# The early expert's remaining tokens as a float32 slot on weights already on chip

## The chip, the cores and the metric

The kernel runs on one core of a Trainium2 chip. The metric is device microseconds of one launch, the median of several runs. The core has five engines with a queue each: TensorE (PE; PEld is its weight load), VectorE (DVE), ScalarE (ACT), GpSimd (POOL) and SyncE (SP, which here only issues DMAs). Each engine works off its queue in order; semaphores between them keep the data right.

## The reference

Three stages follow each other, in float32:

1. Attention: 2 batches, 8 heads, 576 positions, head size 64, softmax over a causal window of 64. Its output, heads side by side, is x with 1152 rows of 512.
2. A mixture of 8 experts. Each token goes to the expert of its largest logit and is weighted by the probability of that choice; an expert takes at most 288 tokens, further ones give zero.
3. A dense layer pair: `h = x @ w_in`, `g = h * clip(h + 3, 0, 6) / 6`, `g @ w_out`, with 2048 hidden columns.

```python
logits = x @ w_gate
expert_idx = np.argmax(logits, axis=1)
...
h = np.maximum(np.einsum('ecd,edf->ecf', disp, w1), 0.0)   # w1: 8 x 512 x 1024
y = np.einsum('ecf,efd->ecd', h, w2)                       # w2: 8 x 1024 x 512
...
    if keep[i]:
        out[i] = gate_w[i] * y[expert_idx[i], pos[i]]
```

## The kernel before

**Early expert.** Attention goes over nine tiles of 128 tokens. After the first five, the expert that holds most tokens so far (the early expert) is chosen (`early_expert`, L722), and up to 128 of its tokens are computed while attention is still going on. Its weights are loaded whole into `wE`: four units of 256 hidden columns, each with a half of w1 and a half of w2 (512 KB each), in float32 as they come. A unit's work is an up product (four matmuls, `early_up`), ReLU on ACT, two transposes of the hidden rows (`early_hidden`), a copy on ACT, and a down product (two matmuls, `early_down`). Units 0 and 1 lie inside attention; units 2 and 3 follow it, in the loop from L1888.

**Slots.** When all tokens are known, the experts are ranked by the tokens they still have (`ranks`, L919; `keyB` takes the early expert's done tokens off its count), and eight slots with fixed capacities take them: ranks 0 to 2 hold 256, 224 and 208 tokens, ranks 3 to 5 hold 128, ranks 6 and 7 hold 64. `RANKS` says which rank each slot has. The early expert's remaining tokens are one of the ranks, and its weights are loaded again like any other's. Tokens are gathered from `x_dram` by GpSimd (`rows_of`, L790), scaled by their gate (`scale`, L1283), turned on TensorE and split into a high and a low part (`prep`).

**Precision.** Slots of 128 tokens and more, and the dense part, use float32r matmuls in three passes (`PASSES`): weights and data are split into high and low parts. Each quarter unit of weights takes a cast on ACT (L253) and a subtraction on DVE (L258). Slots of 64 take the weights as they are. The dense part's weights are converted first (`conv64`, two operations on ACT and four on DVE per piece).

**Stages and order.** The expert stage runs three teams of slots (`TEAMS`), each a large slot (`ws_stage`, weights stationary; a step `w` is half a unit) with one or two small ones (`ts_stage` or `tiny_stage`, steps `a` and `b`); the strings of `ORDER` give the order of the steps. The dense part then goes over four groups of tokens. A slot's finished rows are turned into the dense part's input `x2` by `to_dense`; `x2` has the memory in which `wE` lies before. Loads, casts, subtractions and conversions are jobs that a planner (`advance`, `fill`) puts into the queues wherever its estimates of the engines leave room; a ring of eight raw tiles and a ring of six split halves set how far ahead it goes. `FIRST_AT` and `SECOND_AT` say at which unit the four pieces of the dense part's first two units are loaded and converted. `compact_index` (L1749), which works out where each output row goes, is issued a few operations at a time (`aside`).

**PSUM.** Eight banks; transposes of tokens before the stage take banks 2 and 3 in turn (`t`), the short-lived products of the stage banks 0, 1 and 2 in turn (`rot`).

Of the kernel before, what the change touches and what calls it, by code (L numbers as in the profile page):

```python
# [15 lines left out]
AF = mybir.ActivationFunctionType  # L16
ALU = mybir.AluOpType
# [6 lines left out]
def tile_kernel(ctx, tc, q, k, v, w_gate, w1, w2, w_in, w_out, out, cap):  # L24
# [9 lines left out]

    RANKS = [3, 6, 0, 4, 1, 5, 7, 2]
    TEAMS = [((0, 1), 2), ((3,), 4), ((5, 6), 7)]
    NBIG = 3
    NTINY = 2  # L40
    BIG = (256, 224, 208)
    SCAP = [BIG[r] if r < NBIG else 128 if r < E - NTINY else 64 for r in RANKS]


    PAST = []
    for s, r in enumerate(RANKS):
        for part in range(SCAP[s] // 128, 3 if r <= NBIG else 2):
# [125 lines left out]
    FU = 256  # L173
# [101 lines left out]
    xTE = x2f[:, 2 * NFU * HALF : 2 * NFU * HALF + DM].rearrange("p (c t) -> p c t", c=NC)  # L275


    rt = ctx.enter_context(tc.tile_pool(name="rt", bufs=1))
# [34 lines left out]
    with ExitStack() as actx:  # L313
# [408 lines left out]
        def early_expert(e):  # L722
            ce, (k8, eq, t8, _), (mk, tE) = box["cE"], e8, e1
            at_ = place(0, NE, box["pE"])
            V.scalar_tensor_tensor(out=k8, in0=ce, scalar=8.0, in1=c_desc, op0=ALU.mult, op1=ALU.add)
            next(at_)
            V.tensor_reduce(out=mk, in_=k8, axis=AX.X, op=ALU.max)
            V.tensor_scalar_min(t8, ce, 128.0)
            next(at_)
            V.tensor_scalar(out=eq, in0=k8, scalar1=mk, scalar2=None, op0=ALU.is_equal)  # L730
            V.tensor_copy(et[0], pos[:, 0:NE])
            V.tensor_tensor(out=subE, in0=t8, in1=eq, op=ALU.mult)
            V.tensor_tensor(out=k8, in0=eq, in1=c_e, op=ALU.mult)
            V.scalar_tensor_tensor(out=keyB, in0=subE, scalar=-8.0, in1=c_desc, op0=ALU.mult, op1=ALU.add)
            V.tensor_reduce(out=tE, in_=k8, axis=AX.X, op=ALU.add)
            V.tensor_scalar_mul(nsub, subE, -1.0)
            V.tensor_copy(eI[:, 0:1], tE)
# [111 lines left out]
        def early_hidden_out(u):  # L849
            return lambda e: copy(e, box["hE"][:, early_part(u)], box["vE", u])  # L850
# [99 lines left out]

        def first_gather(e):
            box["x0"] = t = first_w[2]
            rows_of(t, sidx[:, 3 * RANKS[0] : 3 * RANKS[0] + 1])

        def gate_parts(e):
            V.tensor_reduce(out=gate, in_=ex, axis=AX.X, op=ALU.add)
# [877 lines left out]
    def ahead(step, *what):  # L1834
        prep_at.setdefault(step, []).append(what)

    rows_at = []
    for g, (small, b) in enumerate(TEAMS):
        st = start[False, small[0]]
        todo = [(small[0], 0, st - 3), (b, 0, st - 2), (b, 1, st - 1)]  # L1840
        if len(small) > 1:
            todo.append((small[1], 0, st))
        if g == 0:
            todo = [(b, 0, -1), (b, 1, -1), (small[1], 0, 0)]
        for s, i, at_step in todo:
            if g:
                ahead(at_step - 1, prep_scale, s, i)
            ahead(at_step, prep, s, i)
# [22 lines left out]
    xg[0, 0] = box["x0"]  # L1871

    def early_end(u, r):
        r = spend("PE", 0.22, r) + 0.2
        early_hidden(u)("PE")
        fill(r)
        early_hidden_out(u)("A")
        r = spend("A", 0.27, r) + 0.2
        if u >= NFU - 2:
            prep(TEAMS[0][1], u - NFU + 2, "t")  # L1880
        for i in range(2):
            early_down(u, i)("PE")
        r = spend("PE", 1.71, max(r, done["wl", u, 1])) + 0.2
        fill(r)
        return r

    before = None
    for u in range(NEU, NFU):  # L1888
        for i in range(2):
            early_up(u, i)("PE")  # L1890
        r = spend("PE", 1.71, done["wl", u, 0]) + 0.2
        fill(r)
        early_relu(u)("A")
        r = spend("A", 0.27, r) + 0.2
        if u == NEU:
            prep_scale(0, 0, done["g0"])
            prep(0, 0, "t")
            for n, (s, i, _) in enumerate(rows_at[:3]):
                prep_scale(s, i, done["g0"] + 2.2 * (n + 1))
        if before:  # L1900
            early_end(*before)
        before = u, r
    r = early_end(*before)
    early_out("A")
    r = spend("A", 0.52, r) + 0.2
    at(0, to_dense, box["yE"], None, r)
# [68 lines left out]
```

## Time and profile before

| | us |
|---|---|
| runs | 424.16, 425.08, 425.15 |
| median | 425.08 |
| profiled execution | 424.75 |
| its span | 423.0 |
| PE busy | 403.9 (95%) |
| DVE busy | 291.1 (69%) |
| ACT busy | 242.7 (57%) |

The span is the part that the profile covers, from the first instruction to the last; the rest of the execution lies around it. Busy time of TensorE includes the pipeline's modelled ends, so single matmuls overlap: the time that an operation takes of the engine is read from the start of one group to the start of the next. The rows further down are whole lines of the profile; L numbers are lines of this kernel.

### The profile page before, as it was taken

The numbers are of one execution on the slowest core, as the hardware profiler recorded it, in microseconds if no ns is written. First come the engines' busy times: TensorE is split into PE (matmuls) and PEld (weight loads), VectorE is DVE, ScalarE is ACT, GpSimd is POOL, SyncE is SP. The second block draws the span as 40 slices with busy tenths as digits, with TensorE's granted clock in tenths as the row PEclk, the third lists the DMA queues.
The fourth block names the chain that finished last, engine by engine and source line by source line (L and its number), as shares of the span: only waits on it lengthen the run. The fifth ranks groups of instructions, "written<-read, shape, count | busy, mean of one in ns | idle before, by whom it ended". The sixth has DMA issues, their size and how long they took to land.

```text
span 423.0 us, 8492 instructions
## 1 busy us (share of the span) xinstructions
PE 403.9 (95%) x3055; PEld 346.4 (82%) x3055; DVE 291.1 (69%) x801; ACT 242.7 (57%) x526; POOL 51.4 (12%) x108
## 2 busy tenths in 40 slices
PE   8999788889999999999999999999999999999992
PEld 5887665578898999988899999888888888898981
DVE  1988967568989999967679999548896222323430
ACT  3887773576769787736787576348573222422330
POOL 8633404200003001000000000000000000200111
PEclk9999999989999999999999999999999999999998
DMA  9998765997999998699810290032500000110101
GB/s 166 212 234 192 253 249 184 329 356 257 323 322 371 309 308 241 206 339 342 291 65 2 66 331 2 2 99 99 179 24 0 2 0 2 50 50 2 50 27 56
DMA packets 67058, 69.69 MB, mean 165 GB/s; under 512 B 30816, under 2 KB 49248, under 8 KB 67008
## 3 DMA queue, kind: packets, MB, share of 16 engines
q1 hardware_dynamic: 65424, 63.99, 48.4%
q0 software_dynamic: 1584, 5.08, 3.4%
q8 instruction: 26, 0.43, 0.4%
q14 instruction: 24, 0.20, 0.2%
HBM read 64.34 MB, written 4.72 MB: 163 GB/s over the span
## 4 chain that ended last, share of the span: by engine, by line
PE 85%; DVE 5%; DMA 3%; ACT 2%; issue 2%; SPq 1%; POOL 1%; POOLq 0%; ACTq 0%; DVEq 0%
PE banks L239 71%; DMA raw<-in_moe_w_dram 3%; PE banks L496 2%; PE banks L1482 2%; PE banks L1457 2%; PE banks L614 2%; DVE neg L573 1%; PE banks L560 1%; PE banks L596 1%; PE banks L653 1%; PE banks L1419 1%; ACT pe L586 1%; PE banks L1293 1%; PE banks L526 1%; DMA x_dram<-xt 0%
## 5 line engine op out<-in xcount | busy, mean ns | idle before, releaser
L258 DVE TENSOR_TENSOR wt<-raw,wt 128x512 fp32r<-128x512 f32 x116 | 74.9, 685 | 9.2 <-ACT wt L253 8.8
L239 PE MATMUL banks<-x,wt 128*128 128x320 f32 (+3 forms) x432 | 79.8, 336 | 0.0
L239 PEld LDWEIGHTS banks<-x,wt 128*128 128x128 f32 x432 | 70.8, 188 | 7.1
L253 ACT CAST wt<-raw 128x512 fp32r<-128x512 f32 x116 | 68.0, 630 | 9.5 <-DMA raw<-in_moe_w_dram 5.8
L239 PE MATMUL banks<-wt,g 128*128 128x512 f32 x288 | 69.6, 390 | 0.0
L1546 DVE SCALAR_TENSOR_TENSOR gf<-r,banks 128x320 f32<-128x320 f32 (+3 forms) x48 | 26.6, 554 | 60.2 <-ACT r L1543 60.1
L1543 ACT ACTIVATE r<-banks,c_three 128x320 f32<-128x320 f32 (+3 forms) x48 | 28.0, 583 | 68.1 <-PE banks L239 67.8
L239 PEld LDWEIGHTS banks<-wt,g 128*128 128x128 f32 x288 | 53.7, 188 | 10.6
L239 PE MATMUL banks<-xT,wt 128*128 128x256 f32 (+2 forms) x288 | 39.8, 289 | 0.8 <-ACT hf L1413 0.8
L239 PEld LDWEIGHTS banks<-xT,wt 128*128 128x128 f32 x288 | 36.3, 198 | 2.5 <-ACT hf L1413 0.9
L239 PE MATMUL banks<-h,wt 128*128 128x256 f32 (+2 forms) x288 | 37.0, 279 | 0.0
L239 PEld LDWEIGHTS banks<-h,wt 128*128 128x128 f32 x288 | 34.6, 191 | 0.5 <-issue 0.5
L1549 ACT CAST g<-gf 128x320 fp32r<-128x320 f32 (+2 forms) x40 | 21.4, 535 | 15.9 <-DVE gf L1546 15.9
L1552 DVE TENSOR_TENSOR g<-gf,g 128x320 fp32r<-128x320 f32 (+2 forms) x40 | 23.4, 584 | 10.1 <-ACT g L1549 9.4
L1589 POOL DMA_INDIRECT out_dram<-raw,cidx x4 | 3.9, 982 | 206.0 <-DVE raw L1583 198.5
L239 PE MATMUL banks<-x,wt_fixed 128*128 128x320 f32 (+3 forms) x144 | 26.8, 337 | 0.4 <-ACT x L1373 0.4
L239 PEld LDWEIGHTS banks<-x,wt_fixed 128*128 128x128 f32 x144 | 23.5, 188 | 3.0 <-ACT x L1373 0.7
L201 ACT ACTIVATE c<-raw 128x512 f32<-128x512 f32 x32 | 21.5, 673 | 6.5 <-DVE raw L224 4.8
L791 POOL DMA_INDIRECT xg<-x_dram,sidx x10 | 13.5, 1345 | 80.2 <-PE banks L1293 71.5
L239 PE MATMUL banks<-wt_fixed,g 128*128 128x512 f32 x96 | 23.2, 390 | 0.0
L573 DVE CUSTOM_DVE_ANT_0 neg<-banks,tmask 128x128 f32<-128x128 f32 x72 | 16.3, 286 | 9.2 <-POOL c_order L83 7.6
L217 DVE SCALAR_TENSOR_TENSOR c<-raw,c 128x512 uint32<-128x512 uint32 x32 | 22.1, 690 | 0.7
(292 smaller groups left out, 648.5 us busy)
## 6 DMA issues: line engine op xcount, KB each, us to landing
raw<-in_moe_w_dram SPq DMA_DIRECT2D x64, 512.0 KB, 5.7
raw<-in_moe_w_in_dram SPq DMA_DIRECT2D x16, 512.0 KB, 5.3
raw<-in_moe_w_out_dram SPq DMA_DIRECT2D x16, 512.0 KB, 5.3
early<-in_moe_w_dram SPq DMA_DIRECT2D x8, 512.0 KB, 7.5
x_dram<-xt SPq DMA_DIRECT2D x9, 256.0 KB, 3.2
q_sb<-in_q_dram SPq DMA_DIRECT2D x8, 256.0 KB, 4.7
k_sb<-in_k_dram SPq DMA_DIRECT2D x8, 256.0 KB, 4.7
v_sb<-in_v_dram SPq DMA_DIRECT2D x8, 256.0 KB, 4.6
```

The source lines that it names most:

```text
L201: nc.scalar.activation(box["c"].bitcast(F32), box["hi"].bitcast(F32), AF.Abs)
L217: nc.vector.scalar_tensor_tensor(out=box["c"], in0=box["hi"], scalar=0xC0000000, in1=box["c"], op0=ALU.bitwise_and, op1=ALU.bitwise_or,)
L239: nc.tensor.matmul(out, l, r, start=(start and n == 0), stop=(stop and n == len(pairs) - 1))
L253: nc.scalar.copy(hi, r)
L258: V.tensor_tensor(out=lo, in0=r, in1=hi.bitcast(F32), op=ALU.subtract)
L496: nc.tensor.transpose(pt[:, hp, :], t[:, 2 * hp : 2 * hp + 2, :].rearrange("p h d -> p (h d)"), ident)
L573: V.tensor_tensor_reduce(out=neg[:, hp, :], in0=box["sp", g][:, hp, :], in1=tmask[:, first, :], scale=-1.0, scalar=3.0e38, op0=ALU.add, op ...
L791: nc.gpsimd.indirect_dma_start(out=t, out_offset=None, in_=x_dram[0:n], in_offset=bass.IndirectOffsetOnAxis(ap=index.bitcast(U32), axis=0),)
L1543: nc.scalar.activation(r, ph, AF.Relu, bias=c_three)
L1546: V.scalar_tensor_tensor(out=gf, in0=r, scalar=6.0, in1=ph, op0=ALU.min, op1=ALU.mult)
L1549: nc.scalar.copy(hi, gf)
L1552: V.tensor_tensor(out=lo, in0=gf, in1=hi.bitcast(F32), op=ALU.subtract)
```

## The change

The early expert's remaining tokens leave the ranking. Its key is raised so that it always has rank 0 (`keyB` with +128 times its done tokens), and rank 0 is slot 0 with 128 places, which is in no team. The other seven experts have the ranks 1 to 7 with 256, 224, 208, 128, 128, 64 and 64 places. Slot 0 is computed ahead of the expert stage, right behind the early expert's units 2 and 3, in float32 on the weights in `wE`: `rest_turn` scales and turns its rows into `xTR`, `own_up` and `own_end` do a unit, for the early tokens and for the rest alike. The early expert's units 2 and 3 and the rest's four units form one loop; the token turns for the first team (`between`) and three steps of `compact_index` per unit stand inside it. The teams' order and the places of the dense pieces' loads are new.

```diff
-    RANKS = [3, 6, 0, 4, 1, 5, 7, 2]
-    TEAMS = [((0, 1), 2), ((3,), 4), ((5, 6), 7)]
...
+    RANKS = [0, 4, 1, 6, 2, 5, 7, 3]
+    TEAMS = [((1,), 2), ((3,), 4), ((5, 6), 7)]
+    REST = 0
+    CAPS = (128, 256, 224, 208, 128, 128, 64, 64)
+    SCAP = [CAPS[r] for r in RANKS]
...
-            V.scalar_tensor_tensor(out=keyB, in0=subE, scalar=-8.0, in1=c_desc, op0=ALU.mult, op1=ALU.add)
+            V.scalar_tensor_tensor(out=keyB, in0=subE, scalar=128.0, in1=c_desc, op0=ALU.mult, op1=ALU.add)
...
-    FIRST_AT = (3, 4, 4, 7)
-    SECOND_AT = (9, 18, 19, 21)
+    FIRST_AT = (0, 4, 4, 4)
+    SECOND_AT = (7, 7, 17, 19)
...
-    ORDER = ('awwbawbwawbwabww', 'awwawwawwaww', 'awwbawbwaabwbwww')
+    ORDER = ('wwawwawawaww', 'awawwwwawaww', 'awbwwbwaaawbbwww')
...
-            todo = [(b, 0, -1), (b, 1, -1), (small[1], 0, 0)]
+            todo = [(b, 0, -1), (b, 1, -1), (small[0], 0, 0)]
...
+    def rest_turn():
+        x0 = box["x0"]
+        r = scale(x0, 3 * RANKS[REST], done["g0"])
+        pt = quarters(bank("t"))
+        for c in range(NC):
+            nc.tensor.transpose(pt[:, c, :], x0[:, 128 * c : 128 * c + 128], ident)
+        r = spend("PE", 0.43, r) + 0.2
+        fill(r)
+        nc.scalar.copy(xTR, pt)
+        box["rR"] = spend("A", 0.48, r) + 0.2
+
+    def own_up(rest, u):
+
+        key = "uR" if rest else "uE"
+        t = xTR if rest else xTE
+        box[key, u] = bank("rot")[:, 0:FU]
+        mm(box[key, u], [(t[:, c, :], wE[2 * u][:, c * FU : c * FU + FU]) for c in range(NC)])
+        r = spend("PE", 1.83, box["rR"] if rest else done["wl", u, 0]) + 0.2
+        fill(r)
+        nc.scalar.activation(box["hfE"][:, early_part(u)], box[key, u], AF.Relu)
+        return spend("A", 0.27, r) + 0.2
+
+    def own_end(rest, u, r):
+        pt = bank("rot")[:, 0:FU]
+        hf, h = (box[n][:, early_part(u)] for n in ("hfE", "hE"))
+        for kf in range(2):
+            nc.tensor.transpose(pt[:, 128 * kf : 128 * kf + 128], hf[:, 128 * kf : 128 * kf + 128], ident)
...
+        nc.scalar.copy(h, pt)
+        r = spend("A", 0.27, r) + 0.2
+        for fn in between.pop((rest, u), []):
+            fn()
...
+        mm(acc, pairs, start=(rest and u == 0), stop=(u == NFU - 1))
...
+    for rest, u in [(False, u) for u in range(NEU, NFU)] + [(True, u) for u in range(NFU)]:
+        r = own_up(rest, u)
+        if not rest and u == NFU - 1:
+            rest_turn()
+        if before:
+            own_end(*before)
+        if rest:
+            for _ in range(3):
+                next(aside)
+        before = rest, u, r
+    own_end(*before)
+    for step_, key, off_at in ((0, "yE", None), (1, "yR", lambda: off_of(REST))):
+        at(step_, to_dense, box[key], off_at, box[key, "at"])
```

How the engines' queues change shows best in their order of instructions. On TensorE, from the down product of the early expert's unit 1 on, the kernel before has this (`early` are products on `wE`; `first_w_101` are hidden rows, `first_w_103` slot 0's tokens, `xg` the first team's tokens):

```order
L239 MATMUL banks<-early,first_w_102 128x512 x2
L239 MATMUL banks<-early 128x256 x4
L1293 MATMUL banks<-ident,first_w_103 128x128 x4
L239 MATMUL banks<-early 128x256 x4
L845 MATMUL banks<-ident,first_w_101 128x128 x2
L1293 MATMUL banks<-ident,xg 128x128 x4
L239 MATMUL banks<-early,first_w_102 128x512 x2
L845 MATMUL banks<-ident,first_w_101 128x128 x2
L1293 MATMUL banks<-ident,xg 128x128 x4
L239 MATMUL banks<-early,first_w_102 128x512 x2
L239 MATMUL banks<-wt,xT_1554 128x256 x12
```

In the changed kernel the same place reads (the last three rows' pattern goes on through the rest's unit 3):

```order
L238 MATMUL banks<-early,first_w_102 128x512 x2
L238 MATMUL banks<-early 128x256 x8
L1879 MATMUL banks<-ident,first_w_103 128x128 x4
L1900 MATMUL banks<-ident,first_w_101 128x128 x2
L238 MATMUL banks<-early,first_w_102 128x512 x2
L238 MATMUL banks<-early 128x256 x4
L1900 MATMUL banks<-ident,first_w_101 128x128 x2
L238 MATMUL banks<-early,first_w_102 128x512 x2
L238 MATMUL banks<-early 128x256 x4
L1900 MATMUL banks<-ident,first_w_101 128x128 x2
L1295 MATMUL banks<-ident,xg 128x128 x4
L238 MATMUL banks<-early,first_w_102 128x512 x2
```

The up products of units 2 and 3 now follow each other, the turn of slot 0's tokens stands behind both, and between the turn of a unit's hidden rows (L1900) and its down product lies one token turn or nothing.

On VectorE, right behind the gates of all slots (`sgate`), the kernel before has this (`first_w_103` are slot 0's tokens, `xT` the same tokens turned):

```order
L978 SCALAR_TENSOR_TENSOR sgate<-banks,sgate 128x24
L258 TENSOR_TENSOR wt<-raw,wt 128x512 x2
L1285 TENSOR_SCALAR first_w_103<-first_w_103,sgate 128x512
L258 TENSOR_TENSOR wt<-raw,wt 128x512 x2
L1299 TENSOR_TENSOR xT_1554<-banks,xT_1554 128x512
```

In the changed kernel VectorE has this at the same place (`c_1556` is a dense piece in conversion):

```order
L980 SCALAR_TENSOR_TENSOR sgate<-banks,sgate 128x24
L257 TENSOR_TENSOR wt<-raw,wt 128x512 x4
L1287 TENSOR_SCALAR first_w_103<-first_w_103,sgate 128x512
L257 TENSOR_TENSOR wt<-raw,wt 128x512
L207 TENSOR_SCALAR c_1556<-c_1556 128x512
L211 TENSOR_SCALAR c_1556<-c_1556 128x512
L216 SCALAR_TENSOR_TENSOR c_1556<-raw,c_1556 128x512
```

The scaling of slot 0's tokens has moved from behind two weight subtractions to behind four.

On VectorE at the start of the expert stage, up to the first large slot's own subtraction (`h`), the kernel before has this (`x_1614` is the dense input):

```order
L1299 TENSOR_TENSOR xT_1581<-banks,xT_1581 128x4x128
L258 TENSOR_TENSOR wt<-raw,wt 128x512 x3
L1401 TENSOR_TENSOR x_1614<-banks,x_1614 128x4x128
L258 TENSOR_TENSOR wt<-raw,wt 128x512
L1353 SCALAR_TENSOR_TENSOR h<-banks,h 128x256
L1711 TENSOR_TENSOR tns<-rse,cntS 128x64
L1426 TENSOR_TENSOR h<-banks,h 128x256
```

In the changed kernel VectorE comes to that slot's `h` through this (`c_1665` and `c_1686` are dense pieces, `wt_fixed` their split halves):

```order
L1759 TENSOR_TENSOR top_f<-offF,ks 128x8
L216 SCALAR_TENSOR_TENSOR c_1665<-raw,c_1665 128x512
L223 ISA raw<-raw,c_1665 128x512x2
L207 TENSOR_SCALAR c_1686<-c_1686 128x512
L211 TENSOR_SCALAR c_1686<-c_1686 128x512
L216 SCALAR_TENSOR_TENSOR c_1686<-raw,c_1686 128x512
L223 ISA raw<-raw,c_1686 128x512x2
L257 TENSOR_TENSOR wt_fixed<-raw,wt_fixed 128x512 x2
L1355 SCALAR_TENSOR_TENSOR h<-banks,h 128x256
L257 TENSOR_TENSOR wt_fixed<-raw,wt_fixed 128x512
L1403 TENSOR_TENSOR x_1716<-banks,x_1716 128x4x128
```

Where weight subtractions for the stage stood, there are now the conversions of dense pieces and their subtractions, ahead of the first slot's `h` and of the dense input that follows it.

## Rows read from the trace of the kernel before

**Rows 1.** the chain that ended last, in order of time: start us, us, what

```profile
216.83 198.50 PE banks L239 x1006
```

**Rows 2.** busy time by stretch: PE, PEld, DVE, ACT, POOL busy, clock, DMA

```profile
72.70:94.40 21.70, 18.19 (x93) 13.98 (x91) 13.61 (x28) 13.27 (x29) 4.92 (x4) 0.92 1.01 334
94.40:215.90 121.50, 121.50 (x1027) 110.27 (x1026) 105.69 (x240) 87.69 (x193) 6.37 (x4) 1.00 0.89 295
```

**Rows 3.** waits of PE from 72.7 to 94.4 us

```profile
PE banks L239 <- ACT first_w L452: 1.2, 1, 1.2
PE banks L1390 <- ACT first_w L452: 1.1, 1, 1.1
```

**Rows 4.** waits of ACT from 70 to 92 us

```profile
ACT wt L253 <- DMA raw<-in_moe_w_dram: 5.8, 5, 2.8
```

**Rows 5.** busy time by stretch, single microseconds; the clock is third from the end

```profile
79.00:80.00 1.00, 0.79 (x2) 0.49 (x3) 0.00 (x0) 0.64 (x2) 0.63 (x1) 1.00 1.10 292
...
88.00:89.00 1.00, 0.77 (x4) 0.77 (x5) 0.93 (x2) 1.00 (x3) 0.66 (x1) 0.78 1.05 364
...
91.00:92.00 1.00, 1.00 (x7) 1.00 (x6) 0.64 (x3) 0.96 (x3) 0.00 (x0) 0.51 1.07 410
```

**Rows 6.** timeline of PE, 96 to 106 us: start us, us, what

```profile
96.98 1.60 PE L239 MATMUL banks<-wt,xT 128*128 128x256 f32 x12
98.42 1.60 PE L239 MATMUL banks<-h,wt 128*128 128x256 f32 x12
...
102.51 0.44 PE L1419 MATMUL banks<-ident,hf 128*128 128x128 f32 x2
102.88 1.09 PE L1457 MATMUL banks<-raw,xT 128*64 128x128 f32 x16
103.90 1.65 PE L239 MATMUL banks<-wt,h 128*128 128x512 f32 x6
105.39 0.88 PE L239 MATMUL banks<-xT,wt 128*128 128x256 f32 x6
```

**Rows 7.** timeline of PE, 56 to 104 us

```profile
64.16 0.44 PE L845 MATMUL banks<-ident,first_w 128*128 128x128 f32 x2 [0.30 <-ACT first_w L834]
65.06 1.12 PE L239 MATMUL banks<-early,first_w 128*128 128x512 f32 x2 [0.46 <-ACT first_w L452]
...
72.72 1.89 PE L239 MATMUL banks<-early 128*128 128x256 f32 x8
74.45 0.60 PE L1293 MATMUL banks<-ident,first_w 128*128 128x128 f32 x4
...
79.21 1.98 PE L239 MATMUL banks<-early,first_w 128*128 128x512 f32 x4 [1.15 <-ACT first_w L452]
81.03 0.38 PE L845 MATMUL banks<-ident,first_w 128*128 128x128 f32 x2
81.25 0.60 PE L1293 MATMUL banks<-ident,xg 128*128 128x128 f32 x4
```

**Rows 8.** waits of SP from 66 to 80 us

```profile
SPq L1008 <- POOL eofI L1869: 3.0, 1, 3.0
```

**Rows 9.** timeline of DVE, 64 to 104 us

```profile
72.85 0.48 DVE L1285 TENSOR_SCALAR first_w<-first_w,sgate 128x512 f32<-128x512 f32 x1
...
75.63 0.69 DVE L258 TENSOR_TENSOR wt<-raw,wt 128x512 fp32r<-128x512 f32 x1 [1.70 <-ACT wt L253]
...
98.44 0.42 DVE L208 TENSOR_SCALAR c<-c 128x512 f32<-128x512 f32 x1
...
100.20 0.70 DVE L224 CUSTOM_DVE_ANT_0 raw<-raw,c 128x1024 uint16<-128x1024 uint16 x1
```

**Rows 10.** timeline of ACT, 60 to 104 us

```profile
60.03 0.59 ACT L452 COPY early<-banks 128x512 f32<-128x512 f32 x1 [0.28 <-PE banks L806]
```

**Rows 11.** timeline of ACT, 211 to 219 us

```profile
215.72 0.67 ACT L201 ACTIVATE c<-raw 128x512 f32<-128x512 f32 x1
216.28 0.50 ACT L1373 CAST x<-banks 128x416 f32 x1
```

More of the change, by code (lines that the diff above doesn't have):

```diff
@@ L32, in tile_kernel @@
     NC = DM // 128
-    RANKS = [3, 6, 0, 4, 1, 5, 7, 2]
-    TEAMS = [((0, 1), 2), ((3,), 4), ((5, 6), 7)]
[L39 to L42, printed above, removed]
+    RANKS = [0, 4, 1, 6, 2, 5, 7, 3]
[3 more added lines that the diff above has]
+    SCAP = [CAPS[r] for r in RANKS]
     PAST = []
     for s, r in enumerate(RANKS):
-        for part in range(SCAP[s] // 128, 3 if r <= NBIG else 2):
+        for part in range(SCAP[s] // 128, 3 if r <= 4 else 2):
             PAST.append((s, part, max(0, 128 * part - SCAP[s])))
@@ L274, in tile_kernel @@
     wE = [x2f[:, HALF * i : HALF * i + HALF] for i in range(2 * NFU)]
-    xTE = x2f[:, 2 * NFU * HALF : 2 * NFU * HALF + DM].rearrange("p (c t) -> p c t", c=NC)
+    xTE, xTR = (
+        x2f[:, 2 * NFU * HALF + DM * i : 2 * NFU * HALF + DM * i + DM].rearrange("p (c t) -> p c t", c=NC)
+        for i in range(2)
+    )
     rt = ctx.enter_context(tc.tile_pool(name="rt", bufs=1))
@@ L952, in first_gather @@
             box["x0"] = t = first_w[2]
-            rows_of(t, sidx[:, 3 * RANKS[0] : 3 * RANKS[0] + 1])
+            rows_of(t, sidx[:, 3 * RANKS[REST] : 3 * RANKS[REST] + 1])
         def gate_parts(e):
@@ L1847, in tile_kernel @@
                 ahead(at_step - 1, prep_scale, s, i)
-            ahead(at_step, prep, s, i)
+                ahead(at_step, prep, s, i)
             rows_at.append((s, i, at_step))
@@ L1870, in tile_kernel @@
             est["D"] = max(est["D"], spend("P", 0.15) + 0.3)
-    xg[0, 0] = box["x0"]
-    def early_end(u, r):
+    def rest_turn():
[17 more added lines that the diff above has]
+        return spend("A", 0.27, r) + 0.2
@@ L1874, in early_end @@
+    def own_end(rest, u, r):
[3 more added lines that the diff above has]
+            nc.tensor.transpose(pt[:, 128 * kf : 128 * kf + 128], hf[:, 128 * kf : 128 * kf + 128], ident)
         r = spend("PE", 0.22, r) + 0.2
-        early_hidden(u)("PE")
         fill(r)
-        early_hidden_out(u)("A")
+        nc.scalar.copy(h, pt)
         r = spend("A", 0.27, r) + 0.2
-        if u >= NFU - 2:
-            prep(TEAMS[0][1], u - NFU + 2, "t")
@@ L1881, in early_end @@
-        for i in range(2):
-            early_down(u, i)("PE")
-        r = spend("PE", 1.71, max(r, done["wl", u, 1])) + 0.2
-        fill(r)
-        return r
-    before = None
[L1888 to L1899, printed above, removed]
-        if before:
-            early_end(*before)
-        before = u, r
@@ L1903, in tile_kernel @@
[L1903 to L1906, printed above, removed]
+        for fn in between.pop((rest, u), []):
+            fn()
+        if rest and u == 0:
+            box["aR"] = bank("acc")
+        acc = box["aR" if rest else "aE"]
+        pairs = [(h[:, 128 * kf : 128 * kf + 128], wE[2 * u + 1][:, DM * kf : DM * kf + DM]) for kf in range(2)]
+        mm(acc, pairs, start=(rest and u == 0), stop=(u == NFU - 1))
+        r = spend("PE", 1.75, max(r, done["wl", u, 1])) + 0.2
@@ new lines, in own_end @@
+        fill(r)
+        if u == NFU - 1:
+            key = "yR" if rest else "yE"
+            box[key] = y = first_w[2 if rest else 3]
+            nc.scalar.copy(y, acc)
+            box[key, "at"] = spend("A", 0.52, r) + 0.2
+    between = {}
+    for n, (s, i, _) in enumerate(rows_at[:3]):
+        between[True, n] = [
+            lambda s=s, i=i, n=n: prep_scale(s, i, done["g0"] + 2.2 * (n + 1)), lambda s=s, i=i: prep(s, i, "t")
+        ]
+    before = None
+    for rest, u in [(False, u) for u in range(NEU, NFU)] + [(True, u) for u in range(NFU)]:
+        r = own_up(rest, u)
+        if not rest and u == NFU - 1:
+            rest_turn()
+        if before:
+            own_end(*before)
[3 more added lines that the diff above has]
+        before = rest, u, r
```

## The prediction

> **What bounds the kernel now.** I read the chain that ended last first: from 216.83 us it is one unbroken piece of TensorE matmuls, 198.50 us long [rows 1]. That is the dense part, which the change leaves as it is, so a microsecond won or lost ahead of it moves the end by a microsecond. Next come the busy times by stretch [rows 2]. From 94.40 to 215.90 us (the expert stage after its start) TensorE is busy for all of its 121.50 us at clock 1.00: this stage is the sum of its matmuls, and what is taken off VectorE (105.69 us busy) or the DMA (0.89) there is worth nothing by itself. From 72.70 to 94.40 us (the end of the early expert, the start of the stage) TensorE is busy 18.19 of 21.70 us, so 3.5 us are idle, and the granted clock is 0.92. The waits of TensorE in that stretch [rows 3] name ScalarE: copies of the early expert that stood in ScalarE's queue behind weight casts, and these waited 5.8 us for weights to land [rows 4]. The clock by single microseconds [rows 5] is below 1.00 in the four from 88 to 92 us (0.78, twice 0.50, 0.51; 0.50 is 1.2 GHz), just after the waits of 1.1 and 0.8 us: 0.22 + 0.50 + 0.50 + 0.49 = 1.7 us lost. So the stretch holds about 3.5 + 1.7 = 5.2 us that other work could fill. The rest chain goes into exactly this place.
>
> **The change part by part.** I count TensorE time from 72.72 us, where the up product of the early expert's unit 2 starts (nothing ahead of it moves), to the first dense matmul.
>
> Removed: one ranked slot of 128 tokens, slot 0, four units. A unit's starts to starts are 96.98 to 98.42 for the up product (1.44), 102.51 to 102.88 for turning its hidden rows (0.37) and 103.90 to 105.39 for the down product (1.49) [rows 6]. That is 3.30 a unit, 13.2 us in all. It could be as little as 4 x (1.44 + 0.22 + 1.49) = 12.6, with the early expert's turn (below); I take 13.2, the slot's own rows. Its eight loads of 512 KB, 16 casts and 16 subtractions go too, all beside TensorE in a stage without a wait: nothing.
>
> Added: four units in float32. Rows of the same operation are there [rows 7]: unit 2's up product 72.72 to 74.45 (1.73), a turn of hidden rows 81.03 to 81.25 (0.22), a down product 79.21 to 81.03 (1.82). 3.77 x 4 = 15.1 us. Work of the two exchanged: +1.9 us. The Trainium skill, FP8 and Floating Point Precision, section TensorE Precision Notes, says that true float32 takes four passes through the array. By that the up product is 16 passes against 12 and the down product 8 against 6, 4/3 of the slot's 1.44 and 1.49 as an estimate, the four units 16.5 us, and the sum below 4.1 instead of 2.7. The rows lie under it (1.73, 1.82), so they are used.
>
> Moved: three turns of gathered tokens (0.36 us each) are between the rest's units, and the stage has one fewer; the turn of the rest's rows stays, and each finished slot is turned into the dense input as before. Zero. The first dense piece's load is issued third, when SyncE had nothing to do but wait 3.0 us for GpSimd's cast of the expert numbers [rows 8]; the following loads land one place later in the queue, but their casts now stand behind 15 us of new work. Zero, unless ScalarE meets one that has not landed (a rival below). The seven other experts have the same capacities as ranks 0 to 6 or 7 had, so the stage's other products keep their sizes.
>
> New waits in the chain of the rest. It is serial, and the order shown with the change gives what stands between.
> - The turn of the rest's rows waits for their scaling, which VectorE now has behind its fourth weight subtraction. That one ran from 75.63 to 76.32, the scaling takes 0.48 [rows 9], so it ends near 76.8; unit 3's up product, now at once behind unit 2's, ends at 74.45 + 1.73 = 76.2. Wait 0.6.
> - The next turn of hidden rows goes into the PSUM bank that this turn filled, so it waits for ScalarE's copy of 512 columns: 0.59 [rows 10] and the end of the turn, 0.8.
> - A unit's end is turn, copy on ScalarE, down product. With ScalarE free that took 64.16 to 65.06, 0.9 us, of which the turn is 0.22 [rows 7]: 0.7 lost where nothing lies between (early units 2 and 3 and the rest's last one, 2.1), 0.3 where a token turn of 0.36 does (the rest's units 0 and 2, 0.6), and 0.7 at unit 1, whose token turn goes into the bank that the copy still reads. Together 3.4.
> - Backlog of VectorE. Three dense pieces are converted while the rest runs, each from 98.44 to 100.90 in the old trace, about 2.5 us with its four operations [rows 9], and the first steps of the output index are there too. Behind them stand the scaling of two token tiles and the first slot's own subtraction, and two PSUM banks come free only after that. Following the queue by these durations, the two tiles cost 1.2 and the first products of the stage 1.5 more, 2.7 at most; it is nothing if VectorE runs ahead by as much. I take 1.5, nearer to the middle because the first two pieces are spread over work that waits for TensorE.
>
> Waits after: 0.6 + 0.8 + 3.4 + 1.5 = 6.3 us. Before: 5.2. So +1.1: the idle time is filled, and about as much is made anew. I expect the clock to stay at 1.00, since no single gap is over 0.9 us and the wait of 1.2 left it at 1.00 [rows 3, 5]; the gain of 1.7 is in the 5.2.
>
> End of the stage: ScalarE's abs of 0.67 us between the two last copies [rows 11] stands behind both in the new order; the second copy, 216.28 before, can start when its matmuls end. Gain 0.3; the dense part restarts from there.
>
> Sum: +15.1 - 13.2 + 1.1 - 0.3 = +2.7 us. On the profiled execution's 424.75 us (span 423.0, the rest lies around it) this gives 427.45; the median of the runs, 425.08, is 0.3 above that execution, so the time is put at 427.5.
>
> **The rivals.**
> A: no visible change. VectorE has no backlog (1.5 less), and the two bank waits (0.8 and 0.4 of the 0.7) hide behind each other: +2.7 - 2.7 = 0, with half of it +1.3: 424.8 to 426.3. For it: VectorE is busy 13.61 of 21.70 us here [rows 2], there is room. Against it: what fills the room is conversion that is put ahead of what the chain needs.
> B: faster. The place is the same stretch; the mechanism is that ScalarE stops standing before weights that have not landed (5.8 us in the old trace [rows 4]), so that copies come at once and each unit end loses only 0.3. Waits after: 0.6 + 6 x 0.3 = 2.4, against 5.2 before: 15.1 - 13.2 - 2.8 - 0.3 = -1.2, 423.5; with a little off the float32 products 423. It decides when the waits of TensorE from 72.7 us to the first expert product are under 2.5 us in all. Against it: the turn and the copy were 0.9 us long with ScalarE idle.
> C: slower still. A gap in the rest chain grows, because ScalarE meets an unlanded dense piece or casts out of turn, and the clock falls as it did from 88 to 92 us: 1.7 for the clock and about 1 for the gap that sets it off, 427.5 + 2.7 = 430.2. The Trainium skill, TensorE: Matmul & The Clock Gate, section Part 1 (What's actually happening), states that the throttled clock is the default and activity releases it. By that rule a chain full of gaps is at risk; rows 5 agree as to the two levels, and their line from 79 to 80 us, after the longest wait, speaks against it.
> D: the change does not do what it says. If the early expert's rest were over 128 tokens, or a ranked expert over its capacity, the branch for overflow would run, and the dense part once more, 198.5 us [rows 1]. From the reference's inputs the rest is 126, and the other seven are 234, 220, 194, 123, 74, 42 and 11 against 256, 224, 208, 128, 128, 64 and 64: it does not run.
>
> **How the numbers follow.** Forecast 0.50, with its own range 426.4 to 429; A 0.24; B 0.13; C 0.12; D 0.01. About 0.3% of 425.08, 1.3 us, is what a measurement of this kernel can tell from no change: under 423.8 is faster, over 426.4 slower. So faster 0.13, same 0.24, slower 0.63. Range 424.0 to 430.0: the lower end leaves most of B out; the upper end is the sum with the short slot (12.6, +0.6) and the whole backlog (2.7, +1.2), 429.3, and a little of C.
>
> **What would show it.** In the new profile: the stretch from 72.7 us to the first expert product should last some 30 us, with 24 us of work in it and TensorE waits on ScalarE of 0.3 to 0.9 at each unit end; a wait on VectorE at the turn of the rest's rows; one or two waits on VectorE within the first four products of the stage; the clock 1.00 throughout; the dense part again some 198.5 us. The forecast is wrong if the waits sum to under 3 us, if the first dense matmul starts before 216.8 us, or if the stage after its start holds waits of its own.

## The result, and the profile after

| | before | changed |
|---|---|---|
| runs, us | 423.44 to 425.15 (5) | 427.70 to 429.90 (5) |
| median, us | 424.16 | 428.06 |
| ratio | | 1.0094, 95% interval 1.0069 to 1.0120 |
| profiled execution, us | 424.75 | 429.90 |
| its span, us | 423.0 | 428.2 |

The changed kernel is slower by 0.9%, 3.9 us between the medians; 427.5 was forecast, with 424.0 to 430.0 as the range.

The chain that ended last still ends with one piece of TensorE's matmuls, the dense part (start us, us, what). Of before there are 198.50 us behind a break after the first two matmuls [rows 1]; those two are the difference to this line.

```profile
221.49 199.00 PE banks L238 x1008
```

So the time went ahead of it. TensorE's timeline of the changed kernel shows the place (start us, us, engine, line, operation, operands, count; in brackets the idle time before and what ended it), where [rows 6, 7] had slot 0 and the early expert:

```profile
73.34 3.62 PE L238 MATMUL banks<-early 128*128 128x256 f32 x16
77.40 0.66 PE L1879 MATMUL banks<-ident,first_w 128*128 128x128 f32 x4 [0.44 <-DVE first_w L1287]
78.73 0.44 PE L1900 MATMUL banks<-ident,first_w 128*128 128x128 f32 x2 [0.68 <-ACT early L1882]
79.63 3.23 PE L238 MATMUL banks<-early,first_w 128*128 128x512 f32 x4 [0.46 <-ACT first_w L1903]
82.65 2.39 PE L238 MATMUL banks<-early 128*128 128x256 f32 x8
...
85.84 1.98 PE L238 MATMUL banks<-early,first_w 128*128 128x512 f32 x4 [0.58 <-ACT first_w L1903]
...
95.16 0.66 PE L1295 MATMUL banks<-ident,xg 128*128 128x128 f32 x4 [0.58 <-ACT first_w L1903]
...
100.19 0.66 PE L1295 MATMUL banks<-ident,xg 128*128 128x128 f32 x4 [0.72 <-DVE xg L1287]
...
103.30 1.98 PE L238 MATMUL banks<-early,first_w 128*128 128x512 f32 x4 [0.52 <-ACT first_w L1903]
104.72 2.00 PE L238 MATMUL banks<-xT,wt 128*128 128x256 f32 x12
...
108.96 0.66 PE L1392 MATMUL banks<-ident,first_w 128*128 128x128 f32 x4 [0.37 <-DVE h L1355]
110.16 1.69 PE L238 MATMUL banks<-wt,xT 128*128 128x256 f32 x12 [0.54 <-DVE x L1403]
```

Where [rows 3] had waits of 1.2 and 1.1 us on ScalarE, there are ten of 0.3 to 0.7 us. Nine are shown, on the places the prediction named: the scaling of the rest's rows (0.44), ScalarE's copy of them, which holds the PSUM bank (0.68), the copies of hidden rows (0.46, 0.58, 0.58, 0.52), VectorE's backlog at the third token turn (0.72) and at the first products of the stage (0.37, 0.54); the tenth, 0.29, is ahead of the first token turn. The down product at 79.63 lasts 3.0 us to the next start instead of 1.8. The single microseconds (PE, PEld, DVE, ACT, POOL busy, clock, DMA share, GB/s) say why; the clock, third from the end, falls to 0.50 (1.2 GHz) as in [rows 5], and ahead of the last product it does so only here:

```profile
79.00:80.00 1.00, 0.54 (x3) 0.30 (x2) 0.00 (x0) 0.79 (x2) 0.00 (x0) 1.00 1.07 369
80.00:81.00 1.00, 1.00 (x3) 0.32 (x2) 0.32 (x1) 1.00 (x3) 0.00 (x0) 0.62 1.08 357
81.00:82.00 1.00, 1.00 (x3) 0.48 (x2) 0.97 (x3) 0.22 (x1) 0.00 (x0) 0.50 1.06 379
```

0.38 + 0.50 + 0.50 + 0.32 = 1.7 us are lost from 80 to 84 us. By stretch (same columns), from unit 2's up product to the stage's first product, and from there to the dense part, which answers to [rows 2]:

```profile
73.34:104.72 31.38, 27.13 (x101) 16.99 (x100) 20.52 (x58) 17.80 (x37) 4.94 (x4) 0.95 0.79 258
104.72:221.49 116.77, 115.76 (x995) 105.28 (x993) 89.19 (x191) 75.86 (x169) 4.45 (x4) 1.00 0.81 265
```

At the end of the stage both last copies of x are now in one row on ScalarE, without the abs between them [rows 11]; the dense part starts at once, without the wait of 0.4 us it had.

```profile
220.93 1.01 ACT L1375 CAST x<-banks 128x416 f32 x2
```

The two profiled executions differ by 5.15 us: 0.62 lie ahead of unit 2's up product, which the change does not touch, and 4.54 between it and the dense part (148.15 against 143.61, the latter from 72.72 to 216.83 less the 0.50 of the two first dense matmuls).

### The profile page after: what moved, and what is told of

The parts are those of the page before. It is cut to its first block, busy times and chain, and to the rows that moved or that the text cites. A ratio compares the mean times of both kernels' runs of the same rounds, so it can differ in the third digit from the quotient of the medians.

```text
span 428.2 us, 8357 instructions
## 1 busy us (share of the span) xinstructions
PE 406.6 (95%) x3031; PEld 343.7 (80%) x3031; DVE 281.3 (66%) x781; ACT 234.1 (55%) x510; POOL 49.7 (12%) x108
## 4 chain that ended last, share of the span: by engine, by line
PE 84%; DVE 8%; ACT 4%; issue 1%; DMA 1%; SPq 0%; POOL 0%; ACTq 0%; POOLq 0%; DVEq 0%
PE banks L238 71%; PE banks L1459 2%; PE banks L498 2%; PE banks L1484 2%; PE banks L616 2%; ACT pe L588 1%; PE banks L562 1%; DMA v_sb<-in_v_dram 1%; PE banks L598 1%; DVE neg L575 1%; PE banks L1295 1%; PE banks L528 1%; ACT wt L252 0%; DVE raw L223 0%; DVE c L216 0%
## 5 line engine op out<-in xcount | busy, mean ns | idle before, releaser
L257 DVE TENSOR_TENSOR wt<-raw,wt 128x512 fp32r<-128x512 f32 x100 | 64.6, 686 | 17.6 <-ACT wt L252 15.3
L238 PEld LDWEIGHTS banks<-wt,g 128*128 128x128 f32 x288 | 53.7, 188 | 10.6
L252 ACT CAST wt<-raw 128x512 fp32r<-128x512 f32 x100 | 58.8, 629 | 5.4 <-PE banks L238 3.2
L238 PE MATMUL banks<-xT,wt 128*128 128x256 f32 (+2 forms) x288 | 38.4, 283 | 0.0
L238 PEld LDWEIGHTS banks<-xT,wt 128*128 128x128 f32 x288 | 35.0, 192 | 1.9 <-DVE h L1355 0.8
L588 ACT ACTIVATE pe<-neg,nmx 128x128 f32<-128x128 f32 x72 | 22.3, 392 | 0.1
```

The lines of the kernel that those rows point to most:

```text
L238: nc.tensor.matmul(out, l, r, start=(start and n == 0), stop=(stop and n == len(pairs) - 1))
L252: nc.scalar.copy(hi, r)
L257: V.tensor_tensor(out=lo, in0=r, in1=hi.bitcast(F32), op=ALU.subtract)
L588: nc.scalar.activation(pe[:, hp, :], neg[:, hp, :], AF.Exp, bias=nmx[:, hp : hp + 1], scale=-1.0)
```

## The experiments

Ratios are to the kernel before, run on the same chip beside each; its medians were 423.2 to 424.2. The table has the stretches of each profiled execution: "chain" from unit 2's up product to the stage's first product, "stage" from there to the dense part.

| kernel | ratio (95%) | chain | stage | sum, us |
|---|---|---|---|---|
| before | | 10.6 | 133.0 | 143.6 |
| changed | 1.0094 (1.0069 to 1.0120) | 31.4 | 116.8 | 148.2 |
| changed, again | 1.0138 (1.0112 to 1.0165) | 29.7 | 116.8 | 146.4 |
| order | 1.0076 (1.0054 to 1.0098) | 28.8 | 116.7 | 145.5 |
| bank | 1.0068 (1.0047 to 1.0089) | 28.3 | 116.8 | 145.0 |
| scaling | 1.0093 (1.0077 to 1.0108) | 31.5 | 116.8 | 148.3 |
| order and bank | 1.0073 (1.0055 to 1.0090) | 28.4 | 116.7 | 145.1 |
| order and scaling | 0.9981 (0.9970 to 0.9992) | 25.2 | 116.0 | 141.2 |
| all three | 0.9935 (0.9921 to 0.9949) | 24.1 | 115.8 | 139.9 |
| late conversions | 1.0202 (1.0175 to 1.0229) | 28.9 | 121.9 | 150.7 |
| without the rest | 1.0067 (1.0042 to 1.0092) | 16.3 | 128.0 | 144.3 |
| before without slot 0 | 0.9918 (0.9903 to 0.9933) | 8.6 | 129.5 | 138.1 |

The clock takes a part of these stretches: 1.7 us in the chain of "changed", "scaling" and "without the rest", 1.7 in the stage of before, and 3.4 in the stages of "late conversions", "without the rest" and "before without slot 0"; in the other profiles it is at 1.00 there. The two measurements of the changed kernel differ by 0.0044, and the intervals of the versions with one edit overlap the first of them, so a gain of about 1 us is not clear from the ratios: it is read from the sums at clock 1.00, against 146.4.

My theory was the prediction's: the change exchanges 13.2 us of products for 15.1 and fills old waits with as many new ones. The main rival was that VectorE and the order of its queue, not TensorE's products, set the time.

**The order of the products**. `own_end` is cut in two, `own_turn` (turn and copy) and `own_down`.

```diff
-        r = own_up(rest, u)
-        if before:
-            own_end(*before)
...
+        rt_ = own_turn(*before)
+        r = own_up(True, u)
+        own_down(*before[:2], rt_)
```

> The up product of the next unit is issued between a unit's turn of hidden rows and its down product, and the turn of the rest's rows between unit 2's turn and down. Theory L (latency): each unit end of the chain exposes turn, copy on ScalarE, down product; the changed kernel's trace shows these as waits of 0.68, 0.46, 0.58, 0.58 and 0.29 us, 2.6 in all. A product of 1.73 us now covers the copy, so 2.0 to 2.6 go: about 425.8 us (428.1 - 2.3), and the waits on ScalarE's copies of hidden rows are seen once at most, at the rest's last unit (0.5). Rival W (work and backlog): the time of the chain is its float32 work and VectorE's backlog, and a hole that is closed opens at the next token turn or at the stage's first products: within 0.5 of 428.1.

Measured: 426.60 us, 1.0076. The theory's waits went, two others came, and this is the rival's "a hole that is closed opens at the next token turn". TensorE, then VectorE's scaling of the same tiles:

```profile
86.80 0.63 PE L1295 MATMUL banks<-ident,xg 128*128 128x128 f32 x4 [1.54 <-issue]
92.74 0.63 PE L1295 MATMUL banks<-ident,xg 128*128 128x128 f32 x4 [1.65 <-DVE xg L1287]
```

```profile
86.22 0.48 DVE L1287 TENSOR_SCALAR xg<-xg,sgate 128x512 f32<-128x512 f32 x1
92.12 0.48 DVE L1287 TENSOR_SCALAR xg<-xg,sgate 128x512 f32<-128x512 f32 x1
```

Each turn starts as its scaling ends, also the one whose wait is put down to "issue". The scaling had stood behind weight subtractions, a dense piece's conversion and steps of the output index.

**Conversions later**.

```diff
-    FIRST_AT = (0, 4, 4, 4)
-    SECOND_AT = (7, 7, 17, 19)
+    FIRST_AT = (6, 7, 8, 9)
+    SECOND_AT = (11, 13, 17, 19)
```

> Pieces of the dense part's first two units are loaded and converted later (units 6 to 9 and 11 to 19 in place of 0 to 4 and 7 to 19), so that VectorE has no conversion while the rest runs. Theory B (backlog): the three waits on VectorE at the third token turn (0.72) and at the first products of the stage (0.37, 0.54), 1.6 us, go: 426.5 us, and the chain up to the first product of the stage is 0.7 shorter. Rival S: the conversions only change their place, and the stage, where VectorE is busy 87 of 100 parts, gets waits of its own later: 428 to 430. Rival O: the tokens' scaling is held by the operations for the output index instead, the wait of 0.72 stays: 427.2.

Measured: 431.91 us, 1.0202. Both theory B and rival S hold, each in its place. The three waits on VectorE are gone, and the chain is 0.8 us shorter than that of the changed kernel at the same clock (28.9 against 29.7). But in the stage VectorE converts a piece (its rows from 154.19 to 156.44) ahead of the subtraction that TensorE wants:

```profile
155.83 0.69 DVE L223 CUSTOM_DVE_ANT_0 first_w<-raw,c 128x1024 uint16<-128x1024 uint16 x1
156.44 1.89 DVE L257 TENSOR_TENSOR wt<-raw,wt 128x512 fp32r<-128x512 f32 x3
```

```profile
157.18 1.62 PE L238 MATMUL banks<-xT,wt 128*128 128x224 f32 x6 [2.35 <-DVE wt L257]
```

```profile
150.00:170.00 20.00, 17.44 (x136) 15.30 (x133) 13.92 (x31) 10.34 (x22) 0.00 (x0) 0.83 0.77 260
```

Within that wait the clock begins to fall: 0.17 of 20 us, 3.4 us more. The early conversions cost 1.6 us where they are and 5.8 where they were put.

**The bank**.

```diff
+    BANKS["t"] = (3,)
     between = {}
```

> All token turns ahead of the stage go into PSUM bank 3, where they alternated between 2 and 3. Theory L: the turn of unit 2's hidden rows no longer waits for ScalarE's copy of the rest's rows (0.68), and the second token turn no longer for the copy of hidden rows (0.58, of which 0.3 was hidden rows' latency anyway): 0.7 to 1.0 less, 427.2 us. Rival W: both waits were beside other latencies of the same length: 428.1, no change.

Measured: 426.34 us, 1.0068. As theory L has it: the turn of unit 2's hidden rows follows at once, the second token turn too; a part comes back as a longer wait for the copy (0.73 for 0.46).

```profile
77.72 0.38 PE L1900 MATMUL banks<-ident,first_w 128*128 128x128 f32 x2
78.83 1.98 PE L238 MATMUL banks<-early,first_w 128*128 128x512 f32 x4 [0.73 <-ACT first_w L1903]
...
91.92 0.60 PE L1295 MATMUL banks<-ident,xg 128*128 128x128 f32 x4
```

The chain is 1.4 us shorter than in the changed kernel at clock 1.00 (28.3 against 29.7), more than the 0.7 to 1.0 expected: the third token turn's wait is 0.41 shorter as well.

**Without the rest**.

```diff
+    for n, (u, r) in enumerate(((NEU, r2), (NFU - 1, r3))):
+        for fn in between[True, n]:
+            fn()
+        own_end(False, u, r)
...
+    box["yR"], box["yR", "at"] = box["x0"], est["V"]
```

> The rest is not computed at all: its rows go on as gathered and scaled, its four units and the turn of its rows are left out; the three token turns stand between the early expert's last two units. The kernel so has neither slot 0 nor the rest. By the prediction's terms slot 0 was worth 13.2 us of the kernel before and the rest 15.1 us of products, 0.4 of a turn and some 3 us of waits here: 424.2 - 13.2 = 411.0 against before, and 428.1 - 18 = 410 against the changed kernel. Rival: without the rest the stage meets weights, tokens or conversions that are not ready, so the slot (or the rest) had been filling time that is idle otherwise: 413 or more, with waits on ScalarE, VectorE or DMA of 2 us or more before the first products of the stage.

Measured: 425.86 us, 1.0067: 15 us of products less than the changed kernel has, and 1 to 3 us less time. The rival holds, and more strongly than I had written it. The chain is 13.4 us shorter than the changed kernel's at clock 1.00, the stage 11.2 us longer:

```profile
96.58 0.66 PE L1392 MATMUL banks<-ident,first_w 128*128 128x128 f32 x4 [3.40 <-DVE h L1355]
...
118.53 1.65 PE L238 MATMUL banks<-wt,xT 128*128 128x256 f32 x6 [4.11 <-DVE wt L257]
```

```profile
84.00:130.00 46.00, 36.03 (x240) 32.37 (x240) 39.38 (x99) 29.28 (x59) 3.54 (x3) 0.92 0.64 206
```

VectorE is the engine with the least room there, 39.4 of 46 us, with the output index (one piece from 90.94 to 95.50) and conversions ahead of what TensorE waits for. The rest's products gave it time. The clock has its part in this time too: 5.1 us (1.7 in the chain, 3.4 in the stage), and all six executions have a mean clock of 0.974 to 0.982.

**The kernel before without slot 0**.

```diff
-    TEAMS = [((0, 1), 2), ((3,), 4), ((5, 6), 7)]
+    TEAMS = [((1,), 2), ((3,), 4), ((5, 6), 7)]
-    ORDER = ('awwbawbwawbwabww', ...
+    ORDER = ('wwawawwawaww', ...
+    at(14, to_dense, box["x0"], lambda: off_of(0), r)
```

> The kernel before with slot 0 left out (its four units, its loads, casts and subtractions; the rows go on as gathered and scaled), everything else in the order of before, the dense pieces at the same places. The prediction priced slot 0 at 13.2 us of TensorE time in a stage without waits: 13.2 us less, a ratio of 0.969. Rival V: TensorE's work in the first third of the stage covers VectorE's, which has subtractions and conversions to do whether the slot is there or not (16 subtractions of 0.6 fewer, 9.8 us); waits on VectorE take the place of a part of it: 4 to 10 us less only, 0.976 to 0.991. If the ratio is near 1, as when the rest was left out of the changed kernel, it is the supply of weights that sets the stage's end and not its products.

Measured: 420.11 us, 0.9918: 3.7 us less than before, not 13.2, just under rival V's 4 to 10. In the stage that had no wait after its start [rows 2], TensorE now waits for subtractions and casts of weights (engine, tile, line, for whom; us in total, times, longest), and VectorE is busy 21.5 of the 22 us from 108:

```profile
PE banks L239 <- DVE wt L258: 3.9, 5, 1.6
PE banks L239 <- ACT wt L253: 2.0, 2, 1.1
```

```profile
108.00:130.00 22.00, 18.43 (x140) 16.30 (x139) 21.50 (x56) 17.82 (x39) 4.26 (x3) 1.00 0.98 317
170.00:190.00 20.00, 16.61 (x111) 13.14 (x111) 11.64 (x27) 7.83 (x18) 0.00 (x0) 0.83 0.85 280
```

Not all of it is VectorE. The second line has three waits close together, two on ScalarE's casts (0.87, 1.13) and one on a subtraction (1.04), and with them a fall of the clock of 3.4 us; the mean clock of all six executions is 0.987 to 0.990. And ahead of the first line VectorE stood idle for 4.1 us, because ScalarE's cast had waited 3.4 us for weights to land (at 91 us). So the transfers are a rival to VectorE's own work here that no run separates.

**Scaling first**.

```diff
+            rest_turn()
+            for s, i, _ in rows_at[:3]:
+                prep_scale(s, i, done["g0"] + 2.2)
```

> The changed kernel with one edit: the three token tiles are scaled on VectorE right behind the scaling of the rest's rows, where each stood in its own unit end behind weight subtractions, conversions and steps of the output index. Theory B (the prediction's backlog term for the token turns, 1.2 us; 0.72 seen in the trace): 0.7 to 1.2 less than the changed kernel, a ratio of 1.007. Rival: the third turn then waits for ScalarE's copy of hidden rows or its own bank, and what VectorE did not do between comes later, at the first products of the stage: within 0.3 us of the changed kernel, 1.009.

Measured: 427.80 us, 1.0093. The rival is right: less the 1.7 us of the clock the sum is 146.6, as without the edit. The third turn has no wait any more, and the last down product waits longer:

```profile
98.92 0.60 PE L1295 MATMUL banks<-ident,xg 128*128 128x128 f32 x4
...
103.05 1.98 PE L238 MATMUL banks<-early,first_w 128*128 128x512 f32 x4 [1.19 <-ACT first_w L1903]
```

**All three**: order, bank and scaling, and, as a fourth edit, the third token turn in the last unit end.

```diff
+    for n, (s, i, _) in enumerate(rows_at[:3]):
+        between[True, (0, 1, 3)[n]] = [lambda s=s, i=i: prep(s, i, "t")]
...
+    rest_turn()
+    for n, (s, i, _) in enumerate(rows_at[:3]):
+        prep_scale(s, i, done["g0"] + 2.2)
+    own_down(False, NEU, r2)
```

> The first experiment's order (the next unit's up product between a turn of hidden rows and its down product), all token turns in PSUM bank 3, the three token tiles scaled on VectorE right behind the scaling of the rest's rows, and the third token turn in the rest's last unit end. Theory Q (queue order): the waits of the chain are made by what stands ahead on VectorE and ScalarE and by the PSUM bank, not by their total work; the holes of 1.5 and 1.6 us that the first experiment got at its token turns close, and the chain from unit 2's up product to the stage's first product is 26 us (24 of work) where it was 31.4 in the changed kernel and 28.8 in the first experiment: some 3 us less than that one's ratio of 1.0076, about 1.001 of before. Rival V (VectorE's supply): the stage that begins 3 us earlier meets weights and conversions that are 3 us less ready, as when the rest was left out; its waits on VectorE grow by what the chain wins, 1.006 or more.

Measured: 421.24 us, 0.9935 (0.9921 to 0.9949): faster than the kernel before. Theory Q holds, with more than it expected, and rival V falls: the stage that begins 5.6 us earlier has no wait either. One wait is named in chain and stage together, and the products follow each other without a gap (the rest's units 0 and 1 in the third fence).

```profile
PE banks L1879 <- DVE first_w L1287: 0.2, 1, 0.2
```

```profile
72.97:97.09 24.12, 23.82 (x101) 16.21 (x100) 17.24 (x52) 15.37 (x33) 4.43 (x4) 1.00 0.97 326
97.09:212.85 115.76, 115.64 (x995) 105.34 (x994) 92.05 (x197) 78.00 (x174) 4.45 (x4) 1.00 0.82 270
```

```profile
79.45 1.89 PE L238 MATMUL banks<-early 128*128 128x256 f32 x8
81.18 1.88 PE L238 MATMUL banks<-early,first_w 128*128 128x512 f32 x4
82.90 0.38 PE L1900 MATMUL banks<-ident,first_w 128*128 128x128 f32 x2
83.12 1.89 PE L238 MATMUL banks<-early 128*128 128x256 f32 x8
```

**Two of the three.** The first is the version above without the line on the bank, the second the order's version with it; so the second lacks the early scaling and the later third turn.

```diff
-    BANKS["t"] = (3,)
```

```diff
+    BANKS["t"] = (3,)
```

> The fastest version so far without one of its three edits: the token turns alternate between PSUM banks 2 and 3 again; the new order of the products and the early scaling of the tokens stay. Theory Q2 (the two edits need each other: the order uncovers the holes that VectorE's scaling made, 1.5 and 1.6 us; the bank is worth the one wait of 0.6 at the turn of the rest's rows): 0.6 to 1 us more than the version with all three, a ratio of 0.995 to 0.996. Rival: the bank is what opens the chain, as alone it gave more (1.1 us) than the order (0.8) or the scaling (0): 1.000 or more.

> The fastest version so far without another of its edits: the token tiles are scaled each in its own unit end again, behind weight subtractions and conversions, and the third turn is a unit earlier; the new order and bank 3 stay. Theory Q2: the holes of 1.5 and 1.6 us at the token turns are there as in the first experiment, the bank takes 0.6 off: a ratio of 1.005 to 1.007. Rival: with the bank free the scaling is in time, 0.995 or less.

Measured: 422.34 us, 0.9981, and 426.37 us, 1.0073. Without early scaling the holes are there again (1.53 and 1.56 us at the first two token turns), so bank and order together gain no more than either. Its last down product waits 0.70 again, which in the version with all edits the later third turn covers. Without the bank 1.9 us are lost by the ratios, about twice what I expected, and 1.3 by the traces: the turn of the rest's rows waits 0.58 where it waited 0.2 with the bank, the second token turn waits for its bank, and a wait of 0.36 is back at the start of the dense part.

```profile
77.19 0.66 PE L1879 MATMUL banks<-ident,first_w 128*128 128x128 f32 x4 [0.58 <-DVE xg L1287]
...
89.81 0.66 PE L1295 MATMUL banks<-ident,xg 128*128 128x128 f32 x4 [0.53 <-ACT first_w L1893]
```

Order and scaling (with the later third turn, which was not tried by itself) need each other; by the ratios the bank is worth 1.1 us alone, next to nothing beside the order, and 1.9 beside the two others.

**The changed kernel again**.

> The changed kernel, unchanged, on the same chip as the two others. Expected: the ratio of 1.009 again. Its first profile has the clock at half for 3.4 us in the chain of the rest; four other executions had a mean clock of 0.996 or 0.997 and spans 1.6 to 2.2 us shorter. If the fall of the clock is not a fixed part of the change, this profile has the same waits (5 to 5.5 us from 73 to 111 us) at clock 1.00 and a span of about 426.3; if it is, the span is 428 with a clock of 0.992.

Measured: 428.93 us, 1.0138, above what was expected. In part this is the clock: two of its four executions had a mean clock of 0.992 (spans 427.8 and 428.2) and two 0.997 (426.5). The profiled one is of the latter. It has the same waits in the same places, and its clock is 1.00 up to the last product:

```profile
79.00:80.00 1.00, 0.54 (x3) 0.30 (x3) 0.00 (x0) 0.70 (x2) 0.00 (x0) 1.00 1.03 375
80.00:81.00 1.00, 1.00 (x3) 0.40 (x3) 0.23 (x1) 1.00 (x3) 0.00 (x0) 1.00 1.09 362
```

So the fall of the clock is no fixed part of the change. Of ten executions of the changed kernel three have it, by their mean clock of 0.992; their spans are 427.8 to 428.2 us, those of the others 426.0 to 426.7.

## Why the prediction was right, and where it was wrong

**The bound.** Right: the dense part is 199.0 us as before, and whatever was won or lost stood ahead of it.

**The exchange of products.** The version with all three edits has next to no waits, so it shows the products alone. A unit of the rest is 1.73 + 1.72 + 0.22 = 3.67 us there (the last fence of that version), not 3.77; four are 14.7. The stage of before, less its waits (1.06, 0.79 and 0.40) and the 1.7 of the clock, is 129.0 us, and 115.8 in that version: 13.3 less, where 13.2 was predicted, with about 0.4 in it for the token turn that the chain has instead. Both stretches together, less waits and clock, are 138.1 before and 139.7 in that version: the exchange is +1.6. The term of 1.9 was 0.3 too high, since the down product I read had a wait just ahead of it.

**The waits after.** 6.3 us were predicted. At clock 1.00 the changed kernel needs 146.44 us from unit 2's up product to the dense part, the version without waits 139.88: 6.6 more, 5.5 of them in the chain (29.67 against 24.12) and 1.0 at the start of the stage (116.77 against 115.76). This was the largest guess of the working, and its parts are in the trace. The ten waits that the timeline names are only 5.2 us of it: they begin at the modelled end of the matmuls ahead, while the prediction counted from the start of one step to the start of the next. Counted so, the turn of the rest's rows starts 0.6 us after two up products of 1.73 could end, for a predicted 0.6 (scaling); from that turn to the next are 1.33 us, 0.8 more than in the version without waits, for 0.8 (bank); the unit ends at 78.73, 84.88 and 102.41 lose 0.68, 0.74 and 0.67 beyond their turn of 0.22, for 0.7 each; the rest's first unit, with a token turn between, loses 0.6 where 0.3 was put. The backlog's waits are 0.72 + 0.37 + 0.54 = 1.6, for 1.5. With all this the sum against the profiled execution of before is 146.44 - 143.61 = +2.8, where +2.7 was predicted. The signs agree: the chain is 29.7 us at clock 1.00 for "some 30", with 24.1 of work for 24.

**The end of the stage.** The gain of 0.3 fits the wait of 0.40 that is gone in the changed kernel, but no run tests its cause: a wait of 0.36 or 0.37 is back in two experiments (scaling, order and scaling) with both copies in one row as here.

**Luck.** The time itself came out closer than the change. 427.5 is 2.4 us above the median of 425.08 that the forecast started from; with two more runs that median is 424.16, and the change between the medians is 3.9.

**The clock.** Wrong. "I expect the clock to stay at 1.00, since no single gap is over 0.9 us" fails in the first profile, after gaps of only 0.44, 0.68 and 0.46 us. Rival C's fall of the clock is real, but it comes in some executions and not in others. For before this is inferred, since there is only one trace of it: beside the first experiments its executions had mean clocks of 0.991 to 0.997, one of 422.15 us at 0.996 and one of 425.14 at 0.992. The mean also holds a fall behind the last product, which took 1.2 us or more of every span traced here; 0.996 of a span of 420.4 is 1.7 us in all, which leaves no room for a second 1.7. That mis-sized the term of the waits before: I took the 1.7 us of [rows 5] as a sure loss that the change would win back, and the sum started from an execution that had it. Against executions of before without it the change costs more; the 3.9 us between the medians, where these traces give 2.8, fit that. The Trainium skill, TensorE: Matmul & The Clock Gate, section Part 1 (What's actually happening), says of a kernel's start that the number of matmuls at the lower clock varies from run to run of the same kernel. It says so of the start alone; the three executions of ten show such a variation in the middle of a kernel.

**What the reading missed.** "This stage is the sum of its matmuls, and what is taken off VectorE there is worth nothing by itself" is true of the stage as it stood, and slot 0's 13.2 us did come off in the changed kernel (116.8 for 133.0 us with its waits). But it is no price of the slot: left out alone it gave 3.7 us, and the rest left out of the changed kernel 1 to 3, with the clock's losses in both. VectorE is busy for 87 parts of 100 in that stage [rows 2] and has its work in a fixed order; TensorE's products are the time in which it catches up. The change exchanged products for products in nearly the same place, so the two terms could be set against each other; neither could have been used alone. That VectorE's share is the cause is read from the rows of those two kernels, and in the first of them late weights and ScalarE's casts have a part; a run with VectorE's work itself cut was not made.

**The rivals.** A (no change) would have needed the waits to hide behind each other. The scaling experiment shows one doing so (0.72 went, and 0.67 more came at the last down product), but their sum stayed. B was to decide below 2.5 us of waits; there were 5.2 by name. Its mechanism did come: ScalarE waited 5.8 us for weights in five waits [rows 4], and in one wait only in the changed kernel again and in the version with all edits (from 70 to 92 us):

```profile
ACT wt L252 <- DMA raw<-in_moe_w_dram: 2.0, 1, 2.0
```

```profile
ACT wt L252 <- DMA raw<-in_moe_w_dram: 1.8, 1, 1.8
```

That was not enough, since turn and copy cost about 0.7 us a unit without it, as the prediction held against B. With all the edits B's outcome is what happens: 0.2 us of waits and 2.5 us less than before, because a product now covers each copy and the scaling comes in time. D did not happen: no second dense part is in the trace.

## What to carry to other kernels

A serial chain of small steps on several engines was sped up here by putting the next unit's large product between a step and its consumer, but first look who feeds the next wait: by the traces at clock 1.00 order alone gave 0.9 us, early scaling nothing, a bank 1.4, all together 6.6 (6.7 by the ratios). In this stage, with TensorE at 100% and VectorE at 87%, a product was not worth its own time: look at what the next busy engine needs before counting on work removed there. And before a fall of the clock is counted as something to win back, look at whether every execution has it.

## What the runs showed of the hardware

The granted clock fell to 0.50 (1.2 GHz) for 3.4 us after a stretch in which TensorE was busy for 0.60, 0.32 and 0.54 of three microseconds, in one profile of the changed kernel, and did not in another of it with TensorE busy for 0.56, 0.33 and 0.54 of the same three. It also fell within a single wait of 2.35 us in the stage (clock 0.83 over 20 us). A float32 matmul of 128x256 takes 0.43 us (1.73 for 4), a float32r one 0.12 (1.44 for 12, [rows 6]); so here one float32 matmul cost 1.2 times the three of float32r that replace it, not four thirds.
